# A gated spectral filter and Mish block: GpSimd waits for VectorE's two-input operations, x ahead of w1, gated tiles through ScalarE, and a new order of work

## The chip, the cores and the metric

The kernel runs on one core of one Trainium2 chip. Times are device microseconds of a whole execution; the span is the time from the first to the last instruction in the trace and is about 2 us shorter. TensorE is written PE in the profile (PEld is its weight load), VectorE is DVE, ScalarE is ACT, GpSimd is POOL. A run counts as slow when it lies over 1.5% above the fastest of its kernel, and only fast runs go into a ratio.

## The reference

```python
def reference(A_x, A_w_r, A_w_i, B_x, B_w1, B_b1, B_w2, gate_w):   # x is (1, 2048, 512) bf16
    x = A_x
    g = sigmoid((x * gate_w).sum(-1, keepdims=True))
    X = rfft2(x) * (A_w_r + 1j * A_w_i)          # spectral branch
    a = irfft2(X, s=(2048, 512))
    h = x @ B_w1 + B_b1                          # dense branch: 512 -> 1792 -> 512
    b = (h * tanh(softplus(h))) @ B_w2           # Mish
    return g * a + (1 - g) * b
```

(Abridged. The real text has batch dimensions and casts.)

## The kernel before

The whole kernel is one list of tasks (matmul groups, vector operations, transfers) with declared reads and writes. An order string names the tasks in the sequence in which each engine gets them, the engine where there is a choice, and the PSUM slots. Each engine runs its own tasks strictly in that sequence. `place` turns the declared data into semaphore waits. It knows nothing of the ports that VectorE and GpSimd share; the flag `lock=True` on a task is not read by it.

```python
    def place(self, order):
        ...
        pool_last = None
        ...
        for tok in order.split():
            name, eng, slots = (tok + "::").split(":")[:3]
            ...
            if t.eng == "pool" and not t.isdma:      # GpSimd runs behind itself
                if pool_last is not None and pool_last not in t.deps:
                    t.deps.append(pool_last)
                pool_last = t
            self.order[t.eng].append(t)
```

The dense branch runs in four chunks of 512 rows. A chunk has 14 "bias" matmul groups (x times w1, class mm1), a bias add that empties PSUM (on either engine), exp, ln and tanh on ScalarE, then eight multiplies of h by the tanh (two SBUF inputs), then the second matmul (mm2):

```python
    G.any(f"h{c}_{ft}", [("dve", dve(1024), f_h), ("act", 2 * act(512) + 0.18, f_ha, "b_h")], "h", reads=[b, "b1f"], ...)
    ...
    def f_mul(e, a=a, b_=b_, tl=tl, hb=hb):
        v = hs[hb][:, a:b_, 128 * tl:128 * (tl + 1)]
        return e.tensor_tensor(out=v, in0=v, in1=uv_[:, a:b_, 128 * tl:128 * (tl + 1)], op=ALU.mult)

    G.any(f"mul{c}_{fh}_{tl}", [("dve", dve2(n), f_mul), ("pool", pool(n), f_mul, "b_mul")], "mul", lock=True, ...)
```

The filter weights of the spectral branch need 16 copies of 32 partitions by 2064 elements out of a staging area; in the kernel before all 16 stand on GpSimd. The transposed spectrum (task s1r) is later read back over that staging area, so it waits for all of them:

```python
    G.any(f"{nm}m{fh}{pt}{h}", [("pool", 2.03, f_e), ("dve", 0.71, f_e, "b_rev"), ("act", acts(2064), f_a, "b_rva")],
          "w", off=o, lock=True, reads=rd, writes=[key, ("stg", fh, ri, pt, h)], deps=dp)
    ...
    t_s1r.append(dma(f"s1r{g}", rE[g:128:4, 0:8192], scr_r[32 * g:32 * g + 32, :], ..., deps=t_mv))
```

At the end, ten tiles of the spectral result are added to the dense result on VectorE straight from PSUM:

```python
    def f_fin(e, t=t, b=b):
        return e.scalar_tensor_tensor(out=bs[:, t, :], in0=bank(b), scalar=gcol[:, t:t + 1], in1=bs[:, t, :], op0=ALU.mult, op1=ALU.add)
```

The stretch of the order string around the first chunk's multiplies (`mul0`). `wrm`/`wim` with `:pool` are weight copies on GpSimd, and four of them stand in it:

```
wim111:pool tanh0_0 mm1_1_6::1 zcl0 d10::2 d11 wrm100:pool mm1_1_7 ed10:dve p12::0 p13 h1_6:dve s1w2 mm1_1_10::2 wim100:pool mm1_1_11 ep12:dve
mm1_1_8::1 h1_10:act mul0_0_0:dve d12::0 d13 mul0_0_3:dve mm1_1_9 ez0 mul0_0_1:dve tanh0_8 mm2_0_0_0::0 mul0_0_2:dve ed12:dve wrm001:pool mm2_1_0_0::1
```

## Time and profile before

| | before |
|---|---|
| time before the prediction, median of 3 | 154.35 us (154.17 to 154.51) |
| span of the profiled run | 152.6 us |
| mean granted TensorE clock | 0.966 |
| first multiply of chunk 0 | 41.09 us |
| first spectral matmul over the transposed data | 76.72 us |
| first tanh of the last chunk | 130.55 us |

The lines that carry the reading are in the prediction below. One view is not in it: the busy time of each engine by stretch, cut at the three events of the table. The columns are the window and its length, then busy us (and instructions) of PE, PEld, DVE, ACT and POOL, then granted clock, share of the DMA engines, and GB/s. For the kernel before:

```profile
0.00:41.09 41.09, 36.69 (x280) 21.20 (x285) 29.84 (x32) 26.27 (x21) 26.72 (x23) 1.00 0.96 225
41.09:76.72 35.63, 29.64 (x148) 13.90 (x150) 30.59 (x30) 27.14 (x16) 14.67 (x12) 0.86 0.62 206
76.72:130.55 53.83, 50.71 (x363) 28.50 (x369) 52.25 (x78) 51.69 (x39) 0.53 (x2) 1.00 0.30 73
130.55:152.60 22.05, 18.89 (x117) 11.34 (x116) 17.37 (x25) 7.58 (x3) 0.00 (x0) 1.00 0.23 84
```

The second row is the odd one: TensorE, VectorE and ScalarE are all idle for 5 to 8.5 of its 35.63 us, and it alone has a clock under 1.

### The profile page before, as it was taken

The page shows a single profiled execution, that of the slowest core. Times are in us where ns is not written, and L with a number is a line of the kernel's source. Part 1 is how long each engine was busy: PE and PEld are TensorE (multiplying, and loading weights), DVE is VectorE, ACT ScalarE, POOL GpSimd, SP SyncE. Part 2 cuts the span into 40 slices and gives each one's busy share as a digit, 9 for nine tenths or more (in the row PEclk, how much of TensorE's full clock was granted, in tenths as well). Part 3 has the DMA queues.
Part 4 walks back from the last instruction along what each step waited for, and adds up shares of the span by engine and source line. Part 5 has one row for each costly group of instructions (what it writes and reads, how often), then busy time and mean ns, then how long its engine had stood idle before and what let it go on. Part 6 is the DMA issues. An engine that isn't in the chain of part 4 may idle for free.

```text
span 152.6 us, 2289 instructions
## 1 busy us (share of the span) xinstructions
PE 135.9 (89%) x903; PEld 74.9 (49%) x919; DVE 130.0 (85%) x162; ACT 112.7 (74%) x78; POOL 41.9 (27%) x36
## 2 busy tenths in 40 slices
PE   5799999799975389999999999989898799999991
PEld 3554455457522235544466543434654384764471
DVE  0369598996999995858999999999999899999981
ACT  3411469999990959999359999999999999992000
POOL 3150579999999910005000100000000000000000
PEclk9999999999998558999999999999999999999999
DMA  4999999749910397099997556400000000310233
GB/s 123 325 378 336 162 195 131 118 101 291 331 37 0 83 324 292 10 252 391 410 299 180 118 135 161 105 14 0 0 0 4 0 0 0 137 73 0 103 138 105
DMA packets 22830, 22.37 MB, mean 147 GB/s; under 512 B 13668, under 2 KB 19684, under 8 KB 22372
## 3 DMA queue, kind: packets, MB, share of 16 engines
q1 hardware_dynamic: 22496, 22.00, 53.5%
q10 hardware_dynamic: 324, 0.23, 0.6%
q8 instruction: 7, 0.11, 0.3%
q14 instruction: 3, 0.02, 0.0%
HBM read 14.89 MB, written 4.19 MB: 125 GB/s over the span
## 4 chain that ended last, share of the span: by engine, by line
PE 52%; DVE 38%; issue 4%; DMA 3%; ACT 1%; SPq 0%; DVEq 0%
PE ps L925 23%; PE ps L876 17%; DVE hs L909 9%; PE ps L855 5%; DVE rD L883 4%; DVE rD L503 3%; DVE rF L503 3%; DVE rC L757 3%; DMA rA<-in_A_x_dram 3%; DVE tmp L760 3%; DVE rC L503 2%; DVE hs L883 2%; DVE rD L909 2%; DVE rX L942 2%; PE ps L633 1%
## 5 line engine op out<-in xcount | busy, mean ns | idle before, releaser
L876 PE MATMUL ps<-rX,w_sb 128*128 128x512 bf16 x218 | 51.4, 385 | 1.2 <-DVE rC L503 0.5
L925 PE MATMUL ps<-w_sb,hs 128*128 128x512 bf16 (+1 forms) x176 | 41.6, 383 | 7.0 <-DVE hs L909 5.8
L876 PEld LDWEIGHTS ps<-rX,w_sb 128*128 128x128 bf16 x224 | 21.5, 99 | 25.7 <-issue 1.4
L925 PEld LDWEIGHTS ps<-w_sb,hs 128*128 128x128 bf16 x182 | 17.8, 101 | 26.4 <-DVE hs L909 6.9
L897 ACT ACTIVATE uT<-hs 128x2048 bf16<-128x2048 bf16 (+1 forms) x12 | 20.4, 1696 | 13.0 <-DVE hs L883 7.1
L899 ACT ACTIVATE uT<-uT 128x4096 bf16<-128x4096 bf16 (+1 forms) x8 | 25.5, 3191 | 0.1
L900 ACT ACTIVATE uT<-uT 128x4096 bf16<-128x4096 bf16 (+1 forms) x8 | 25.5, 3190 | 0.1
L883 DVE TENSOR_TENSOR hs<-ps,b1f 128x1024 bf16<-128x1024 f32 x15 | 17.9, 1213 | 2.5 <-PE ps L876 2.4
L909 DVE TENSOR_TENSOR hs<-hs,uT 128x1024 bf16<-128x1024 bf16 (+1 forms) x24 | 19.5, 872 | 0.1
L942 DVE TENSOR_SCALAR rX<-ps,omg 128x512 bf16<-128x512 f32 (+1 forms) x16 | 11.4, 711 | 6.6 <-PE ps L925 6.6
L925 PE MATMUL ps<-w_sb,rD 128*128 128x512 bf16 x53 | 12.9, 379 | 1.5 <-DVE rX L942 0.8
L503 DVE CAST rC<-ps 128x1024 bf16<-128x1024 f32 x9 | 10.9, 1213 | 2.0 <-PE ps L622 1.8
L503 DVE CAST rD<-ps 128x1024 bf16<-128x1024 f32 x8 | 10.3, 1305 | 1.7 <-PE ps L633 1.6
L506 ACT ACTIVATE rC<-ps 128x1024 bf16<-128x1024 f32 x7 | 6.9, 1027 | 4.2 <-PE ps L743 4.2
L503 DVE CAST rA<-ps 128x1024 bf16<-128x1024 f32 x7 | 8.8, 1299 | 0.1
L925 PEld LDWEIGHTS ps<-w_sb,rD 128*128 128x128 bf16 x56 | 5.2, 98 | 7.1 <-DVE rX L942 1.3
L669 POOL TENSOR_SCALAR rW<-rE 32x2064 bf16<-32x2064 bf16 x4 | 8.1, 2024 | 1.4 <-DMA rE<-in_A_w_r_dram 1.0
L608 DVE TENSOR_TENSOR rB<-rA 128x1024 bf16<-128x1024 bf16 (+2 forms) x7 | 4.0, 589 | 5.3 <-DMA rA<-in_A_x_dram 5.3
L506 ACT ACTIVATE rX<-ps 128x512 bf16<-128x512 bf16 x8 | 4.6, 596 | 5.3 <-PE ps L595 5.3
L668 POOL COPY rA<-rE 32x2064 bf16<-32x2064 bf16 x4 | 8.3, 2076 | 0.3
L608 POOL TENSOR_TENSOR rB<-rA 128x1024 bf16<-128x1024 bf16 (+1 forms) x3 | 5.0, 1667 | 11.6 <-DMA rA<-in_A_x_dram 11.6
L669 POOL TENSOR_SCALAR rA<-rE 32x2064 bf16<-32x2064 bf16 x4 | 8.0, 1991 | 0.3
(83 smaller groups left out, 173.1 us busy)
## 6 DMA issues: line engine op xcount, KB each, us to landing
scr<-rD SPq DMA_DIRECT2D x4, 512.0 KB, 4.2
rF<-c_m SPq DMA_DIRECT2D x1, 2048.0 KB, 9.5
rE<-scr SPq DMA_DIRECT2D x4, 512.0 KB, 5.7
rB<-c_g SPq DMA_DIRECT2D x1, 2048.0 KB, 10.4
tmp<-rC SPq DMA_DIRECT2D x16, 128.0 KB, 2.3
out_dram<-rX SPq DMA_DIRECT2D x7, 256.0 KB, 2.0
rA<-in_A_x_dram SPq DMA_DIRECT2D x3, 512.0 KB, 9.3
w_sb<-in_B_w_dram SPq DMA_DIRECT2D x2, 768.0 KB, 9.3
```

Of the source, the lines that this page charges most:

```text
L503: return e.tensor_copy(out=o(), in_=i())
L506: return e.activation(o(), i(), AF.Copy)
L608: return e.tensor_tensor(out=xu[:, a:b_, uv, :], in0=x_sb[:, a:b_, 0:256], in1=x_sb[:, a:b_, 256:512], op=ALU.add if uv == 0 else ALU.subt ...
L669: return e.tensor_scalar(out=o_, in0=i_, scalar1=1.0, scalar2=0.0, op0=ALU.mult, op1=ALU.add)
L876: ins = e.matmul(bank(b, i), w1_sb[:, dt_, 128 * ft:128 * (ft + 1)], xT[:, c, dt_, :, :], start=(dt_ == 0), stop=(dt_ == 3))
L883: return e.tensor_tensor(out=hs[hb][:, ft:ft + 2, :], in0=pair(b).rearrange("p (f s) -> p f s", f=2), in1=b1f[:, ft:ft + 2].unsqueeze(2).t ...
L897: return e.activation(o, hsf[hb][:, 512 * a:512 * b_], fn_)
L899: return e.activation(o, o, fn_, bias=1.0)
L900: return e.activation(o, o, fn_)
L909: return e.tensor_tensor(out=v, in0=v, in1=uv_[:, a:b_, 128 * tl:128 * (tl + 1)], op=ALU.mult)
L925: ins = e.matmul(bank(b)[:, 0:hi - lo], hs[hb][:, ft, 128 * tl:128 * (tl + 1)], w2_sb[:, ft, lo:hi], start=(ft == 0), stop=(ft == NFT - 1))
L942: return e.tensor_scalar(out=bs[:, t, lo:hi], in0=bank(b)[:, 0:hi - lo], scalar1=omg[:, t:t + 1], scalar2=None, op0=ALU.mult)
```

## The change

Its intent is to keep GpSimd and VectorE from needing their shared ports at the same time, to feed the spectral branch earlier, and to take work off VectorE at the end. The order string was made anew to go with it, so it differs nearly everywhere. Cut to its core:

```diff
@@ place
-        pool_last = None
+        pool_last = lock_last = None
...
                 pool_last = t
+                if lock_last is not None and lock_last not in t.deps:
+                    t.deps.append(lock_last)
+                lock_last = None
+            if t.eng == "dve" and t.lock:
+                lock_last = t
@@ ORDER (both strings cut to the multiplies of chunk 0)
-... mul0_0_0:dve d12::0 d13 mul0_0_3:dve mm1_1_9 ez0 mul0_0_1:dve tanh0_8 mm2_0_0_0::0 mul0_0_2:dve ed12:dve wrm001:pool ...
+... mul0_0_0:dve mm1_1_11 mul0_0_2:dve mul0_0_3:dve mm2_0_0_0::0 mul0_0_1:dve mul0_1_1:dve exp1_0 mul0_1_0:dve ... mul0_1_3:dve mm2_0_0_1 h1_10:dve mul0_1_2:pool ...
+... wim101:dve ... wrm011:dve ... wim001:dve ... wim111:dve ... wim010:pool ... wrm001:dve ...
@@ loads
-        ld_x(0); ld_x(1); ld_w1(0); ld_x(2); ld_w1(1); ld_w1(2); ld_x(3); ld_x(4)        # one call a line in the kernel
+        for s in LOADS[loads].split():          # loads=1: "x0 x1 x2 w0 w1 x3 w2 x4"; x0..x2 are x tiles 0 to 7
+            (ld_x if s[0] == "x" else ld_w1)(int(s[1]))
@@ gated tiles (merge: 10 -> 12 tiles kept apart; finb=11 of them in the new way)
+                    if t < finb:
+                        G.add(f"fa{t}", "act", ..., lambda ...: e.activation(tb(z)[:, 0:512], bank(b), AF.Copy, scale=gcol[:, t:t + 1]), ...)
+                        G.any(f"fb{t}", [("pool", pool(512), f_fb), ("dve", dve2(512) + 0.03, f_fb, "b_fb")], ..., lock=True, ...)   # bs += tmp
+                    else:
                         G.add(f"fin{t}", "dve", dve(512) + 0.06, f_fin, "fin", ...)
```

By the new order string, five of the sixteen weight copies run on VectorE, seven more bias adds run on VectorE rather than ScalarE, five output scalings go the other way, six two-input operations move from VectorE to GpSimd, and ten of the eleven gated adds go to VectorE and one to GpSimd.

## The prediction

> **What bounds the kernel now.** I read the page's busy shares and slices first. No engine is full over the whole span (PE 89%, VectorE 85%, ScalarE 74%), so the bound changes by stage, and the slices say where to look: the granted clock falls in one place only.
>
> ```profile
> PE 135.9 (89%) x903; PEld 74.9 (49%) x919; DVE 130.0 (85%) x162; ACT 112.7 (74%) x78; POOL 41.9 (27%) x36
> ...
> PEclk9999999999998558999999999999999999999999
> ```
>
> A slice is 152.6 / 40 = 3.8 us, so the digits 8, 5, 5, 8 cover about 46 to 61 us. I then took the chain of waits around it:
>
> ```profile
> 41.13 8.62 DVE hs L909 x4
> ...
> 51.84 1.65 DVE gcol L730
> ...
> 54.10 5.05 PE ps L925 x12
> ```
>
> Four VectorE multiplies (the activation times tanh, 128x1024 each) take 8.62 us, and a 12-column multiply takes 1.65 us. The timeline of VectorE has the same four multiplies in the last chunk, and the timeline of GpSimd shows what differs:
>
> ```profile
> 41.09 8.66 DVE L909 TENSOR_TENSOR hs<-hs,uT 128x1024 bf16<-128x1024 bf16 x4
> ...
> 134.20 2.50 DVE L909 TENSOR_TENSOR hs<-hs,uT 128x1024 bf16<-128x1024 bf16 x4
> ```
> ```profile
> 42.34 4.56 POOL L668 COPY rA<-rE 32x2064 bf16<-32x2064 bf16 x2
> 46.98 2.23 POOL L669 TENSOR_SCALAR rA<-rE 32x2064 bf16<-32x2064 bf16 x1
> 49.28 4.20 POOL L668 COPY rW<-rE 32x2064 bf16<-32x2064 bf16 x2
> ```
>
> At 134 us GpSimd is empty and the four take 2.50 us. At 41 us GpSimd runs its filter-weight copies, 1.90 us each when undisturbed; each multiply then takes about one such copy more, and the copies stretch to 2.1 to 2.3 us. The two engines take turns. The waits say who pays:
>
> ```profile
> PE ps L925 <- DVE hs L909: 5.8, 2, 3.1
> ACT uT L897 <- DVE hs L909: 5.5, 2, 3.7
> ```
>
> TensorE stands for 5.8 us and ScalarE for 5.5 us. Afterwards TensorE runs at half clock: the 12 matmuls at 54.10 take 5.05 us, 421 ns each, against 14 in 3.02 us (216 ns each) in the chain at 141.10, at full clock.
>
> **What the Trainium skill says.** "SBUF — State Buffer", section "Who interferes with whom", says that a VectorE instruction with two SBUF inputs contends with a GpSimd instruction that reads SBUF, that whoever issues first holds the shared ports for the whole instruction, and that a VectorE instruction with one SBUF input outside the two-port modes doesn't contend. The trace agrees: the bias adds (PSUM and one small SBUF operand) take 1.20 us at 31.41, beside GpSimd copies, and 1.22 us at 80.62 with GpSimd idle. "TensorE: Matmul & The Clock Gate", section "Why this matters for your kernels", asks for no PE gap above about 3 us; the gaps here are 2.72 and 3.11 us and the clock did fall to 0.50 (49.7 to 54.0 us). "GPSIMD Engine Reference", section "Engine selection", calls two-input work about twice as slow on GpSimd; for this bf16 shape the trace says 2120 ns against 681 to 685 ns, three times. "VectorE: DVE Perf Modes", section "The perf-mode tier table", gives bf16 copies in SBUF four elements per cycle; the trace has 1.24 us for 64x4160.
>
> **The change part by part.**
>
> *The semaphore wait.* Each GpSimd instruction now waits for the last VectorE two-input (or weight) operation placed before it. That does not by itself stop a later VectorE operation from running into a GpSimd one; it is the new order that does. After nearly every GpSimd read of SBUF it puts about 2 us of VectorE work that reads PSUM (two bias adds, for instance), as long as the GpSimd instruction lasts. Ten weight copies stand on GpSimd before the first multiply: from 19.9 us (the weights' landing, about unchanged) 10 x 1.97 = 19.7, to about 40 us; the first multiply comes at about 41 us. Of the six left, five go to VectorE: 2064 / 4160 of 1.24 us with its fixed part, about 0.7 us each, 3.4 us together (an estimate; the odd row length is not in this trace).
> Worth: multiplies 8.66 - 2.50 = 6.2 us; the small operations at 50.88 and 51.84, 0.66 + 1.65 less two of 0.16, 2.0 us. That is 8.2 us on VectorE. On TensorE it is idle 2.72 + 3.11 = 5.8, plus half clock (5.05 - 12 x 0.216 = 2.5, and 2.64 - 8 x 0.216 = 0.9): 9.2 us. VectorE heads the chain and TensorE follows; I count 9 us, and take 1 us back for collisions that remain.
>
> *Who does what.* Counted from the order, with durations from start to start (bias add 1.14, spectral evictions 1.14 to 1.22, output scaling 0.66, 1024-column multiply 0.605, 768-column 0.48). VectorE: +7 bias adds (+8.0), +5 copies (+3.4), +2 inverse evictions (+2.3), -3 forward evictions (-3.5), -5 output scalings (-3.3), -6 two-input operations to GpSimd (-3.4), and gated adds below (-2.4): about +1 us, from some 120 uncontended to 121. ScalarE up to its last tanh: 7 bias adds away (7 x 1.17 = -8.2), two inverse evictions away (-1.9), three forward ones in (+2.9), five output scalings in (+3.0), one gated tile (+0.6): -3.6 us. ScalarE has no idle over 0.2 us from 80.98 to 138 except 0.2 at 104.4, so this is worth having only because VectorE can take it: 2 to 3 us. Also the forward spectrum is finished before the first multiply rather than at 63.7 us, so ScalarE's 3.90 us wait at 77.8 for the next spectral matmuls should shrink: 1 us.
>
> *x tiles 0-7 ahead of w1.* x landed to 0.5 MB at 5.56 us, and 1.5 MB (x0, x1, w1 first part, x2) at 8.85 us. With x2 and w1 swapped, x2 lands near 7 and w1 near 8.9, where the first bias matmuls began (8.82). TensorE does four transposes and two spectral tiles in that time and isn't interrupted by transposes at 18.5 to 23.5. Some 0.5 us later for the first exp, about 2 us of ScalarE copies moved out of the exp stage into its idle 8.1 to 14.8: near 0 in sum.
>
> *Gated tiles.* The words say GpSimd adds them; the order gives 10 of the 11 adds to VectorE. Each replaces a 0.67 us PSUM operation by a ScalarE copy (0.6) and a 512-column SBUF add, about 0.36 us (from 0.605 and 0.48): 9 x 0.31 less, one gone to GpSimd, hence -2.4 with one tile kept as before and one more tile. ScalarE has room: it stands idle from 138 us on. But from 135.3 to 149.6 us TensorE is full (14.2 us for the last four tiles and nine spectral products, 65 x 0.216 = 14.0), and it has 15 us of such work in the new order. So this part is worth nothing at the very end, 0 to 1 us before it.
>
> Sum on the span: 152.6 - 9 + 1 - 2.5 - 1 - 0.5 = 140.6. Timed runs lie 1.75 us over the span (154.35 against 152.6): 142.4, say 142.5 us.
>
> A check by VectorE alone: from 41 us to the last chunk's first multiply it has about 75 us of work in the new order; at before's idle share in the same stretch (some 8%) that is 81, so 122; TensorE's 15, a bubble of 0.6 and the output's 3 us make 140.6.
>
> **The rivals.** (1) VectorE becomes the bound and eats it: it gets the bias adds and copies, while its busy share was already 16.8 of 17 us from 87 to 104. If the weight copies run at one element per cycle (about 2.2 us), they cost 7.5 us more in the very stretch that is to be freed, and the time would be 148 to 150. For: odd rows of 129, reversed. Against: the 1.24 us row. (2) The wait moves: GpSimd, held back, finishes the weights later, and the read of the transposed spectrum, which overwrites their staging, waits. Before, that read was issued at 64.2 us; by my count the last weight is done near 55 us, so there are 9 us of slack. If it bites: 145 to 147. (3) The contention was hidden: everything after 60 us is limited by transfers or TensorE anyway. Against: TensorE was busy 14.8 of 15 us from 72 to 87, and transfers idle from 104 to 120. Then 150 to 154. (4) The slower start: w1's first part at 11 us instead of 9 would cost 1 to 2 us.
>
> **Range and chances.** All three engines meet the last chunk within about 2 us of each other in my count, so stalls add rather than hide; a better packed order could also give 139. Range 138 to 148. Over 2% faster means under 151.3, which needs only a third of the contention to come back: 0.92; within 2%: 0.06; slower: 0.02.
>
> **What would show it.** Right: the first chunk's multiplies at 0.6 us each, no granted clock below 0.9 after the start, PE's wait for the multiplies under 1 us, GpSimd copies at 1.9 us, VectorE copies of weights at 0.7 us, the last tanh some 12 us earlier than 136.96. Wrong: a multiply still near 2 us, weight copies over 1.2 us on VectorE, the spectral matmuls waiting on the read of the transposed spectrum, or a TensorE gap of 3 us elsewhere with the clock falling again.

## The result, and the profile after

The changed kernel took 143.94 us (median of 4 runs, 143.0 to 145.94, the highest of them slow) against 154.43 us for the kernel before in the same rounds (4 runs, 154.17 to 154.82). A ratio here is the mean time of one kernel's fast runs over that of the other's fast runs of the same rounds, so not quite the ratio of the medians: it is 0.9298, with a 95% interval of 0.9247 to 0.9349. All outputs were correct, here and in every run below. The predicted 142.5 us (138 to 148) holds the result.

From the page of the changed kernel, the busy shares, the granted clock and the chain of waits:

```profile
PE 133.1 (94%) x917; PEld 74.5 (52%) x917; DVE 123.7 (87%) x161; ACT 116.2 (82%) x81; POOL 42.0 (30%) x39
...
PEclk9999999999999999999999999999999999999999
...
PE 72%; ACT 20%; DMA 3%; DVE 1%; issue 1%; SPq 0%; ACTq 0%
```

The dip in the clock is gone, and VectorE has all but left the chain that ends last; its share there was 38% before. The same stretches as before, cut at the same three events:

```profile
0.00:43.62 43.62, 38.96 (x323) 23.82 (x324) 33.63 (x35) 28.75 (x22) 25.27 (x23) 1.00 1.05 240
43.62:68.60 24.98, 24.98 (x117) 11.31 (x116) 23.71 (x32) 24.53 (x13) 6.64 (x9) 1.00 0.72 225
68.60:118.51 49.91, 48.97 (x359) 27.77 (x358) 48.75 (x67) 47.86 (x33) 8.89 (x7) 1.00 0.33 83
118.51:141.80 23.29, 20.15 (x124) 11.55 (x121) 17.56 (x30) 15.01 (x15) 1.15 (x1) 1.00 0.25 91
```

Row by row the lengths differ by +2.53, -10.65, -3.92 and +1.24 us, which is -10.8 in all. Some work has moved between the rows with the new order, so they are a guide and not a proof, but the second row speaks clearly: TensorE is busy for all 24.98 us of it, where it had been idle for 6 and at half clock for part of the rest. VectorE's timeline and then GpSimd's show why (start, us, engine, line, operation, and in brackets the idle time before it and what ended that; the line numbers shift by a few between kernels because the text above them grew):

```profile
43.62 4.07 DVE L912 TENSOR_TENSOR hs<-hs,uT 128x1024 bf16<-128x1024 bf16 x7
...
50.07 0.70 DVE L671 COPY rA<-rE 32x2064 bf16<-32x2064 bf16 x1
...
54.87 0.16 DVE L733 TENSOR_TENSOR gcol<-ez,omg 128x12 f32<-128x12 f32 x1
```
```profile
38.15 3.91 POOL L672 TENSOR_SCALAR rA<-rE 32x2064 bf16<-32x2064 bf16 x2
47.83 1.64 POOL L912 TENSOR_TENSOR hs<-hs,uT 128x768 bf16<-128x768 bf16 x1 [5.77 <-DVE hs L912]
53.06 1.91 POOL L672 TENSOR_SCALAR rA<-rE 32x2064 bf16<-32x2064 bf16 x1 [3.58 <-DVE rA L672]
```

Seven multiplies take 4.07 us (0.58 each). GpSimd stands still for 5.77 us just then, released by the last of them; it starts at 47.83, while VectorE empties PSUM. The small operation that took 1.65 us takes 0.16. A weight copy takes 0.70 us on VectorE and 1.91 on GpSimd. One collision remains, in the third chunk: three 768-column multiplies that start at 101.83 us take 2.68 us beside a GpSimd multiply that started at 101.52, where four of them take 1.96 at 127.27 with GpSimd empty. The gain can be read again near the end, on ScalarE. These are the tanh operations of the last chunk, first of the kernel before, then of the changed one:

```profile
130.55 6.41 ACT L900 ACTIVATE uT<-uT 128x4096 bf16<-128x4096 bf16 x2
```
```profile
118.51 3.62 ACT L903 ACTIVATE uT<-uT 128x4096 bf16<-128x4096 bf16 x1
...
124.48 2.75 ACT L903 ACTIVATE uT<-uT 128x3072 bf16<-128x3072 bf16 x1
```

The first half starts 12.0 us earlier. The second ends at 127.23 instead of 136.96, 9.7 us earlier, because the new order puts an eviction, an output scaling and a gated tile (1.30 + 0.67 + 0.69 us by the timeline) between the halves.

### The profile page after: what moved, and what is told of

It is laid out like the page before. It is cut to its first block, busy times and chain, and to the rows that moved or that the text cites. A ratio compares the mean times of both kernels' runs of the same rounds, so it can differ in the third digit from the quotient of the medians.

```text
span 141.8 us, 2331 instructions
## 1 busy us (share of the span) xinstructions
PE 133.1 (94%) x917; PEld 74.5 (52%) x917; DVE 123.7 (87%) x161; ACT 116.2 (82%) x81; POOL 42.0 (30%) x39
## 4 chain that ended last, share of the span: by engine, by line
PE 72%; ACT 20%; DMA 3%; DVE 1%; issue 1%; SPq 0%; ACTq 0%
PE ps L879 34%; PE ps L928 26%; ACT uT L900 5%; ACT uT L902 5%; ACT uT L903 5%; DMA rA<-in_A_x_dram 3%; PE ps L746 3%; PE ps L625 2%; PE ps L636 2%; PE ps L954 2%; ACT rD L515 2%; PE ps L598 2%; PE ps L716 1%; DVE rD L512 1%; ACT L903 1%; ACT L902 1%
## 5 line engine op out<-in xcount | busy, mean ns | idle before, releaser
L928 PE MATMUL ps<-w_sb,hs 128*128 128x512 bf16 (+1 forms) x182 | 39.3, 363 | 0.0
L886 DVE TENSOR_TENSOR hs<-ps,b1f 128x1024 bf16<-128x1024 f32 x21 | 25.2, 1219 | 1.9 <-PE ps L879 1.7
L912 DVE TENSOR_TENSOR hs<-hs,uT 128x1024 bf16<-128x1024 bf16 (+1 forms) x22 | 12.2, 616 | 0.4 <-ACT uT L903 0.3
L945 DVE TENSOR_SCALAR rX<-ps,omg 128x512 bf16<-128x512 f32 (+1 forms) x11 | 7.6, 701 | 3.6 <-PE ps L928 3.4
L512 DVE CAST rC<-ps 128x1024 bf16<-128x1024 f32 x8 | 9.6, 1217 | 0.4 <-PE ps L625 0.3
L962 ACT ACTIVATE tmp<-ps,gcol 128x512 bf16<-128x512 f32 x11 | 7.1, 685 | 3.1 <-PE ps L954 2.4
L966 POOL TENSOR_TENSOR rX<-rX,tmp 128x512 bf16<-128x512 bf16 x1 | 1.2, 1152 | 27.8 <-ACT tmp L962 27.8
L512 DVE CAST rF<-ps 128x1024 bf16<-128x1024 f32 x8 | 9.1, 1208 | 0.0
L886 DVE TENSOR_TENSOR rD<-ps,b1f 128x1024 bf16<-128x1024 f32 x7 | 8.4, 1219 | 0.5 <-PE ps L879 0.5
L512 DVE CAST rD<-ps 128x1024 bf16<-128x1024 f32 x6 | 7.5, 1305 | 1.0 <-PE ps L636 1.0
```

What stands on the lines that cost most here:

```text
L512: return e.tensor_copy(out=o(), in_=i())
L886: return e.tensor_tensor(out=hs[hb][:, ft:ft + 2, :], in0=pair(b).rearrange("p (f s) -> p f s", f=2), in1=b1f[:, ft:ft + 2].unsqueeze(2).t ...
L928: ins = e.matmul(bank(b)[:, 0:hi - lo], hs[hb][:, ft, 128 * tl:128 * (tl + 1)], w2_sb[:, ft, lo:hi], start=(ft == 0), stop=(ft == NFT - 1))
L945: return e.tensor_scalar(out=bs[:, t, lo:hi], in0=bank(b)[:, 0:hi - lo], scalar1=omg[:, t:t + 1], scalar2=None, op0=ALU.mult)
L962: G.add(f"fa{t}", "act", act(512) + 0.09, lambda e, t=t, b=b, z=z: e.activation(tb(z)[:, 0:512], bank(b), AF.Copy, scale=gcol[:, t:t + 1]) ...
```

## The experiments

Twelve experiments ran, with nine different kernels, in three calls. All kernels of a call share a chip and the runs of the kernel before.

My theory was that collisions on the shared ports cost some 9 us, that the new order (and not the wait) removes them, and that moved work gives 2 to 3 us more. The rival explanations were: the wait removes the collisions and the order adds little; the moved work is the gain; or the earlier x loads are.

In the first call the kernel before had a median of 154.17 us in seven runs (151.74 to 154.97). One run at 151.74 makes all the others count as slow by the 1.5% rule, so there is no ratio for this call; I compare the medians within it and say where the choice matters.

### 1. The changed kernel again

No edit: it is the base line of the call.

> The changed kernel itself, for a reference on this chip. Expected 143 to 145 us, as before; no granted clock under 0.9 after the start.

Measured: 143.52 us (142.69 to 144.42), 10.65 below the kernel before of the same call. The first result stands.

### 2. The old order with the wait alone

```diff
 # kernel before; ORDER, loads and gated tiles untouched
-        pool_last = None
+        pool_last = lock_last = None
...
                 pool_last = t
+                if lock_last is not None and lock_last not in t.deps:
+                    t.deps.append(lock_last)
+                lock_last = None
+            if t.eng == "dve" and t.lock:
+                lock_last = t
```

> The kernel before with the semaphore wait alone, its old order kept. My prediction says that the order and not the wait keeps the engines apart: then most of the loss stays, 149 to 153 us, multiplies of the first chunk still near 2 us. Rival: in the old order too ten weight copies end before the first multiply, and the wait alone holds the eleventh back until the fourth multiply is done: then the four take 2.5 us, the clock stays up, and nearly all of the 9 us come back, 145 to 147 us.

Measured: 145.49 us (144.63 to 146.07), 8.7 below the kernel before (6.3 below its one run at 151.74) and only 2.0 above the changed kernel. By medians a few lines of `place` do four fifths of the work, which is what the rival that credits the wait says. VectorE's timeline, then GpSimd's, of this kernel:

```profile
40.04 2.50 DVE L914 TENSOR_TENSOR hs<-hs,uT 128x1024 bf16<-128x1024 bf16 x4
...
43.66 0.94 DVE L732 TENSOR_SCALAR gcol<-ez 128x12 f32<-128x12 f32 x1
```
```profile
42.67 1.90 POOL L673 COPY rW<-rE 32x2064 bf16<-32x2064 bf16 x1 [3.14 <-DVE hs L914]
47.08 3.87 POOL L673 COPY rA<-rE 32x2064 bf16<-32x2064 bf16 x2 [2.51 <-DVE hs L914]
```

The four multiplies take 2.50 us where they took 8.66, to the hundredth what the prediction read from the last chunk. GpSimd's idle time before each of its copies ends with a multiply: it is held for 3.14 and 2.51 us and then runs undisturbed (1.90 us) beside VectorE's evictions from PSUM. In the kernel before, the eleventh copy had started at 40.38 us, ahead of the first multiply at 41.09, though it stands behind the four multiplies in the order string: nothing held it. The wait does not keep a later VectorE operation from running into a copy, and one does (0.94 us rather than 0.16), but that costs 0.8 us, not 8. All 16 copies stay on GpSimd here and are still done at 57 us. So my sentence that the wait "does not by itself stop" the collisions and that "it is the new order that does" is refuted in its second half. The start must be set apart: in this run the first bias matmuls were at full clock from 8.8 us (0.22 to 0.25 us apart, against 0.43 in the trace of before), so the first exp came 1.0 us earlier and with it the first multiply. From the first multiply to the end it is 103.1 us here and 111.5 in the kernel before: the wait is worth 8.5 us there.

### 3. The new order without the wait

```diff
 # changed kernel, order and all else kept
-                if lock_last is not None and lock_last not in t.deps:
-                    t.deps.append(lock_last)
-                lock_last = None
-            if t.eng == "dve" and t.lock:
-                lock_last = t
```

> The changed kernel without the semaphore wait, its new order kept. If the order alone does it: 143.5 to 145 us, the first chunk's multiplies at 0.6 us. If the wait is needed as well: GpSimd's multiply of the first chunk starts at 46.2 us with VectorE's and each takes turns (some 1.6 us lost), and its three filter products start as soon as their data land and cost VectorE up to 2 us each: 146 to 150 us.

Measured: 151.05 us, in four runs of 149.66, 152.45, 147.71 and 153.07; the two highest count as slow. By medians that is 3.1 below the kernel before. Fast runs against the one fast run of the kernel before it is 3.1 as well (148.7 against 151.74), and 5.2 above the changed kernel (143.5). VectorE's timeline of this kernel, then GpSimd's:

```profile
44.84 7.22 DVE L907 TENSOR_TENSOR hs<-hs,uT 128x1024 bf16<-128x1024 bf16 x7
...
85.69 2.40 DVE L761 TENSOR_TENSOR rC<-rC,tmp 128x1024 bf16<-128x1024 bf16 x1
```
```profile
47.46 2.00 POOL L907 TENSOR_TENSOR hs<-hs,uT 128x768 bf16<-128x768 bf16 x1 [3.56 <-ACT uT L898]
49.55 2.10 POOL L667 TENSOR_SCALAR rA<-rE 32x2064 bf16<-32x2064 bf16 x1
```

Without the wait GpSimd is released by the tanh instead of by the multiplies, falls into the middle of them, and the seven take 7.22 us instead of 4.07. A filter addition at 85.69 takes 2.40 us instead of 0.69, beside a GpSimd multiply at 85.57. The order alone does not keep the engines apart. The scatter of 5.4 us fits that small shifts in time decide whether two operations meet, but I have the trace of only one of the four runs, so that is argued and not shown.

The medians of this kernel are too scattered to say how far the two parts overlap. The traces say more, from the first multiply to the end (table after experiment 4): without the wait the old order takes 8.5 us longer than with it, the new order 4.2 us (102.4 against 98.2). So in the one run traced the new order by itself avoids about half of the loss.

### 4. The five weight copies back on GpSimd

```diff
 # changed kernel, order string
-... zcl0 wim101:dve ... wrm011:dve s1w3 wim001:dve ... wim111:dve ... wrm001:dve ...
+... zcl0 wim101:pool ... wrm011:pool s1w3 wim001:pool ... wim111:pool ... wrm001:pool ...
```

> The changed kernel with its five VectorE weight copies given back to GpSimd. VectorE has 3.5 us less to do; GpSimd ends its copies near 61 us instead of 55, so the read of the transposed spectrum is issued at about 62 us instead of 58.4. If there is slack as I predicted (first spectral matmul at 68.6 us unmoved): 143 to 144.5 us. If the read bites: the first spectral matmul at 70 to 72 us and the time 145 to 148 us.

Measured: 151.26 us (150.3 to 151.55), 7.7 above the changed kernel of the call. VectorE's timeline, then TensorE's:

```profile
60.63 1.24 DVE L684 TENSOR_SCALAR rA<-rA 64x4160 bf16<-64x4160 bf16 x1 [1.81 <-POOL rA L672]
65.64 1.24 DVE L683 COPY rW<-rW 64x4160 bf16<-64x4160 bf16 x1 [3.77 <-POOL rW L671]
```
```profile
68.85 1.74 PE L879 MATMUL ps<-rX,w_sb 128*128 128x512 bf16 x4 [4.01 <-DVE rD L886]
...
76.59 0.61 PE L746 MATMUL ps<-rE,rF 128*128 128x128 bf16 x8
```

The duplications of the weights (64x4160) stand early in VectorE's sequence and wait for GpSimd's copies. The bias adds behind them wait too, TensorE gets no free PSUM for 4.01 us, and its next matmuls start 435 ns apart (1.74 / 4), half clock (the trace records 0.50 from 69.0 to 72.5 us). The first spectral matmul comes 8.0 us later than in the changed kernel. Of these, 2.1 were lost before the first multiply (45.73 against 43.62), where nothing was edited: in this run the first bias matmul came at 13.03 us and the clock record begins at 14.43, against 11.37 and 10.79. The copies account for the other 5.9 in this trace. So the five moves are needed by this order, and the trace shows the wait in VectorE's own sequence. The read of the transposed spectrum is late too (issued at 65.63 instead of 58.36), so the second rival of the prediction, with its "9 us of slack", was set aside on a count that holds only for the copies as placed; what the late read would cost by itself no run shows. In the old order with the wait all 16 copies fit on GpSimd.

The kernels of the call and the kernel before side by side (us into the profiled run; then the span, the part of it from the first multiply on, and the median time):

| | first multiply | first spectral matmul | first tanh, last chunk | span | from first multiply | time |
|---|---|---|---|---|---|---|
| before | 41.09 | 76.72 | 130.55 | 152.6 | 111.5 | 154.17 |
| wait only | 40.04 | 66.77 | 121.16 | 143.1 | 103.1 | 145.49 |
| order and the rest, no wait | 44.84 | 72.54 | 123.93 | 147.3 | 102.4 | 151.05 |
| both | 43.62 | 68.60 | 118.51 | 141.8 | 98.2 | 143.52 |
| both, copies on GpSimd | 45.73 | 76.59 | 126.50 | 149.8 | 104.1 | 151.26 |

(The traces of before and of both are those of the first result; the profiled run of the changed kernel in this call differs by at most 0.2 us in these events.) The column from the first multiply on is the steadiest measure: the first result and experiments 1, 5, 6, 9, 10, 11 and 12 have the same order from the first multiply on, and in all eight traces it takes 98.21 to 98.23 us. So in these eight runs all the difference in span lies before the first multiply. In the old order with the wait the first spectral matmul even comes earlier than in the new one, 66.77 against 68.60, because the new order reaches its first multiply 3.6 us later. From the first multiply on the new order is 4.8 us shorter, most of it (4.5) between the first spectral matmul and the last chunk's tanh.

### 5 and 10. The first bias matmuls ahead of the transposes of x tiles 4 to 7

```diff
 # changed kernel, loads=2 ("x0 x1 w0 x2 w1 x3 w2 x4") and the head of the order string
-... evx1:act bf4_1:dve wr1s0 p2::2 p3 tr7::0 ... tr4::1 ... tr6::0 p4::0 ... tr5::1 ... tr_b::0 ... mm1_0_2::1 ...
+... evx1:act wr1s0 p2::2 p3 ep0:dve tr_b::0 ... mm1_0_0::0 ... mm1_0_1 ... mm1_0_2::1 tr7::1 ... tr4::0 ... tr6::1 ... tr5::0 p4::0 p5 ...
```

> The changed kernel with another start: w1's first part is loaded ahead of x tiles 4-7, and the first bias matmuls stand before the transposes of tiles 4-7 and their spectral tiles on TensorE. If those transposes, paced by ScalarE's evictions, are what moved the first bias matmul from 8.8 to 11.4 us, it starts near 9 us, and as TensorE heads the chain up to 98 us some 1 to 2.4 us come off: 141 to 142.5 us. If the later start is made good elsewhere anyway: 143 to 144 us.

> The kernel with the early first bias matmuls again. Its first five bias matmuls started 0.4 us apart (half clock), which ate the early start. Expected the same as before, 142.3 to 143.3 us, 0.5 to 1.2 us under the changed kernel.

Measured: 142.79 us (141.51 to 143.62) in the second call, ratio 0.9257 (0.9204 to 0.9309), where the kernel before had 154.49; and 143.63 us (143.21 to 144.42) in the third, ratio 0.9343 (0.9302 to 0.9385), beside the changed kernel at 145.6 there (experiment 9). In the third call that is 2.0 us by medians and 1.5 by the ratios, whose intervals just miss each other. TensorE's timeline of the changed kernel, then of this one:

```profile
11.37 12.26 PE L879 MATMUL ps<-rX,w_sb 128*128 128x512 bf16 x56
```
```profile
8.81 3.76 PE L879 MATMUL ps<-rX,w_sb 128*128 128x512 bf16 x12
```

The first bias matmul comes 2.56 us earlier and the first exp 1.4 (16.58 against 18.02), but the first chunk's matmuls end at 23.24 instead of 23.46 us and the first multiply starts at 43.40 instead of 43.62. In the third call it is the same: 43.67 against 43.79, and the two profiled runs took 143.81 us each. So the traces show 0.1 to 0.2 us; the rest of the difference comes from the other five runs of the changed kernel in that call (144.83 to 146.27), which left no trace. The transposes that the changed kernel does first have to be done in either case, and the early matmuls are slow: twelve take from 8.81 to 12.40, 299 ns each, against 216 ns for the 56 in the line above it (23.46 less 11.37, over 56). The view gives a granted clock of 1.00 throughout, but the traces of experiments 5 and 10 hold no clock record at all; the spacing of the first six (0.40 to 0.43 us) says that it was half.

### 11. The same with 15 warm-up matmuls instead of 9

```diff
 # kernel of experiment 10
-        NWARM = 9
+        NWARM = 15
```

> The same with 15 warm-up matmuls instead of 9 (TensorE is idle there until x lands at 5.5 us). If the slow first bias matmuls are the clock that hasn't come up, they start 0.216 us apart, the first chunk's bias matmuls end about 1 us earlier (22.2 instead of 23.2 us) and the time is 0.5 to 1 us less, 141.5 to 142.5 us. If they wait for w1's landing: no change.

The Trainium skill ("TensorE: Matmul & The Clock Gate", section "What's actually happening") says that the warm-up is a matter of time, about 3.4 us, and not of the number of matmuls. In the changed kernel the nine take 2.10 us, in this one the fifteen take 3.38. TensorE's timeline of this kernel:

```profile
8.22 2.76 PE L879 MATMUL ps<-rX,w_sb 128*128 128x512 bf16 x11
```

Measured: 141.79 us (141.46 to 141.85, 4 runs), ratio 0.9215 (0.9175 to 0.9255), 3.8 below the changed kernel's median of the same call and 1.8 below experiment 10. The order has twelve matmuls here (one record is missing), and they take from 8.22 to 10.82, 217 ns each. The first multiply starts at 41.80 instead of 43.62 and the last chunk's tanh at 116.71 instead of 118.51: 1.8 us won at the start are kept to the end. Its clock record begins with 1.00 at 4.96 us, 3.8 us after the first warm-up matmul; in the changed kernel it begins at 10.79. This agrees with the page, and it shows that the slow early matmuls of experiment 5 were an unwarmed clock. It is the best version, ahead of both kernels. The longer warm-up without the early bias matmuls was not tried, so the share of each in the 1.8 us is not separated beyond what experiment 10 shows.

### 6 and 12. The load order alone

```diff
 # changed kernel, loads=2: w1's first part before x tiles 4 to 7
-... braw ident x2 graw w1_0 w1_1 x3 ...
+... braw ident graw w1_0 x2 w1_1 x3 ...
```

> The changed kernel with only x tiles 4-7 and w1's first part swapped back in the load order, the instruction order kept. If the load order is worth what I predicted (near 0): 143.5 to 144.3 us, the first bias matmul at 11.4 to 12 us. If x's early landing is what the new start rests on: 1 us or more later, 144.5 to 146 us.

> The changed kernel with only the load order of x tiles 4-7 and w1's first part swapped back, again, since its six runs spread over 3.4 us. If the load order costs by itself: 1 to 1.8 us over the changed kernel of this call. If that was scatter: within 0.7 us of it.

Measured: 145.31 us (143.84 to 147.2; three of six runs slow), ratio 0.939 (0.9316 to 0.9464); and 144.33 us (143.72 to 146.85), ratio 0.9388 (0.9343 to 0.9432), where the changed kernel of the same call has 0.9438 (0.9386 to 0.949). The intervals overlap: the swap of the two loads by itself cannot be told from nothing. The profiled runs show how uneven the start is. The first bias matmul came at 11.57 us in the one and at 13.19 us in the other of these two runs of the same kernel, the transposes of the late x tiles having started at 9.02 and 9.54 us. Eight of them take 0.62 us in the one and 1.03 in the other, so part of the difference is again a clock that was warm in one run and not in the other (the record of the second begins at 13.34 us; the first has none). What makes the landing of x and the early clock vary from run to run stays open.

### 9. The changed kernel a third time

No edit: the base line of the third call.

> The changed kernel once more, so that the three runs beside it are compared on one chip: 143 to 144.5 us.

Measured: 145.6 us (143.81 to 146.27), ratio 0.9438 (0.9386 to 0.949), with the kernel before at 153.69. On this chip the gain is 5.6%, on the first 7.0%. The size of the gain is known to about one and a half percentage points across chips.

### 7. The gated tiles on VectorE as before

```diff
 # changed kernel, finb=0: each fa in the order becomes fin, and each fb goes
-... fa10::0 mul3_0_1:dve ... fa4::1 fb10:dve ... fb0:pool ...
+... fin10 mul3_0_1:dve ... fin4 ...
```

> The changed kernel with the gated tiles as before, one VectorE operation out of PSUM each in the place of the ScalarE copy. Mine: TensorE is full at the end, so it is worth 0 to 1 us: 143.5 to 144.6 us. Rival: the 3 us less on VectorE all count, 146 us and more.

Measured: 145.86 us (144.94 to 146.42), ratio 0.945 (0.9402 to 0.9498). There was no changed kernel in this call. Against its ratios in the other calls (0.9298 and 0.9438) the loss is between 0.2 and 2.3 us, so the time alone does not size it; the trace does. First from its waits between 122 and 150 us (what waits and for what, us in total, times, longest), then from VectorE's timeline:

```profile
PEld ps L953 <- DVE rX L957: 1.9, 4, 1.1
...
PE ps L953 <- DVE rX L957: 0.6, 1, 0.6
```
```profile
134.44 3.38 DVE L957 SCALAR_TENSOR_TENSOR rX<-ps,gcol,rX 128x512 bf16<-128x512 f32 x5
```

VectorE works the gated tiles off one behind the other at 0.66 us, and TensorE's products for the next tiles wait for the PSUM that they hold. From the first tanh of the last chunk to the end it is 24.8 us (118.93 to 143.7) against 23.3 in the changed kernel: 1.5 us. The timed runs lie 2.3 to 2.5 us over their spans here and 1.8 to 2.1 in the changed kernel, so some 0.5 us more is lost outside the span. In the changed kernel's own waits of that stretch this wait does not appear.

### 8. The seven bias adds back on ScalarE

```diff
 # changed kernel, order string: seven tasks
-h1_12:dve h1_10:dve h1_8:dve h2_8:dve h3_10:dve h3_6:dve h3_4:dve
+h1_12:act h1_10:act h1_8:act h2_8:act h3_10:act h3_6:act h3_4:act
```

> The changed kernel with seven bias adds given back to ScalarE (1.17 us each, 8.2 us). Mine: ScalarE heads the chain up to the last tanh, so most of it shows, 146 to 150 us. Rival: VectorE, 8 us lighter, is the tighter engine: 142 to 144 us.

Measured: 149.81 us (149.18 to 150.44), ratio 0.971 (0.9653 to 0.9768). ScalarE's timeline of this kernel:

```profile
125.38 3.62 ACT L903 ACTIVATE uT<-uT 128x4096 bf16<-128x4096 bf16 x1
```

The last chunk's first tanh comes 6.9 us later than in the changed kernel, and the span is 6.9 us longer (148.7 against 141.8). Seven bias adds at the 1.17 us that the prediction took from the kernel before are 8.2 us, so nearly all of it lands on the end: in this order ScalarE's sequence sets most of the time up to the last tanh. The figure holds for this order: the old order with the wait has those adds on ScalarE and is only 2 us slower in all.

## Why the prediction was right, and where it was not

**The collisions and their price: right.** The sum put 9 us less 1 on them. The wait alone brings 8.7 us by medians and 8.5 from the first multiply to the end of the traces, with the multiplies at 2.50 us for four as read from the last chunk, the small operations at 0.16 but for one, and no gap over 1 us and no half clock on TensorE in that stretch (its 512-column matmuls stay 0.22 us apart; the trace has no clock record).

**Which part removes them: wrong.** The step that failed is "That does not by itself stop a later VectorE operation from running into a GpSimd one; it is the new order that does." The first clause holds as a statement about what the wait can do, but it was taken for the size of the effect. In the old order the six copies that collided all stand behind the four multiplies and had only run ahead of their place, so holding them back was enough (experiment 2: 8.5 us), and the new order without the wait still loses 4.2 us in its trace (experiment 3). I had looked for what could still go wrong after a GpSimd instruction started, and not at which instructions had started before their turn. The total came out right because both parts were in the change.

**Who does what: right in direction, the parts mis-sized.** I took VectorE's busy time from some 120 uncontended to 121; it is 122.7 with the wait alone and 123.7 in the changed kernel, so the difference of 1 holds. Everything but the wait is worth 2.0 us beside it by medians (145.49 to 143.52), where the terms of the sum, - 2.5 - 1 - 0.5, gave 4.0. By the traces it is worth 4.8 us from the first multiply on, and a start that is 3.6 us later gives most of that back (part of the 3.6 is the early clock of experiment 2's run). The bias adds alone are worth more than the 2 to 3 us (6.9 in the trace of experiment 8, in this order), so the other moves cost something too.

**Weight copies on VectorE: right in cost, for the wrong reason.** They take 0.70 us each, as estimated, so the first rival is out. Without those moves this order loses 5.9 us after the first multiply (experiment 4), through the operations that queue behind the copies on VectorE. The read of the spectrum, the second rival, is 7.3 us late there too, so the slack that I counted is gone; whether it alone would have bitten is not shown.

**x ahead of w1 and the start: mis-sized.** I had 0.5 us later for the first exp and near 0 in sum. The first exp starts at 18.02 us instead of 14.80, 3.2 us later, and the first multiply 2.5 us later. The weights too reach GpSimd at 22.24 us and not at the 19.9 that I took as unchanged. The load order by itself cannot be told from nothing (experiments 6 and 12). Putting the first bias matmuls ahead of the four transposes moves the first multiply by 0.1 to 0.2 us in the traces (experiments 5 and 10); with a warm clock as well it moves by 1.8 (experiment 11). I had not looked at the clock of the start at all. What makes up the rest of the later start is open. So the fourth rival, a slower start, came true beside the gain.

**Gated tiles: mis-sized.** I had "nothing at the very end, 0 to 1 us before it"; the trace of experiment 7 gives 1.5 us, and it lies after the first tanh of the last chunk. I had counted TensorE as full there and VectorE's time as free. In a full stretch TensorE still needs empty PSUM, and who empties it sets its pace.

**The tests.** Multiplies at 0.6 us, no clock under 0.9 after the start, GpSimd copies at 1.9 and VectorE copies at 0.7 all held, and TensorE no longer waits for the multiplies in the changed kernel. The last tanh is 9.7 us earlier, not 12, for the work put between its halves.

## What to carry to other kernels

Where two engines share a port, ask which instructions of one stand behind the other's burst in the order and are yet free to start before it: one wait that holds them behind the burst may give nearly all the gain, and it can be tried alone before any reordering. A copy moved between two in-order engines changes what stands behind it in both sequences, so count the operations that queue behind its consumer, and not only the transfer that waits for it. Compare runs from a fixed event on as well as by their totals: here that took the uneven start out of the comparison. An earlier start on TensorE was worth 0.2 us with a cold clock and 1.8 with a warm one, and in a stretch where TensorE is full the engine that empties PSUM sets the pace.

## What the Trainium skill lacked or had wrong

- "GPSIMD Engine Reference", section "Engine selection", gives about twice VectorE's time for two-input work. For 128x1024 bf16 operands the trace of the changed kernel has 1.97 us on GpSimd (at 82.95 us, undisturbed) against 0.69 on VectorE, close to three times, so the figure does not hold for this shape and type.
- "TensorE: Matmul & The Clock Gate", section "Seeing it yourself", warns that throttle events in a trace can be unreliable. It does not say that they can be missing: five of the fourteen traces here (experiments 2, 5, 6, 8 and 10) hold none, and the view then prints 1.00, for experiment 5 too, whose first matmuls started 0.40 to 0.43 us apart. Where there are records they fit the spacing: in the kernel before it falls from 0.43 to 0.22 us at 10.95 us, and the record begins at 10.97.
- "TensorE: Matmul & The Clock Gate", section "Why this matters for your kernels", sets the limit of a gap at about 3 us. Here a gap of 2.72 us in the kernel before (it ended at 47.50) was already followed by a clock of 0.50 from 48.5 us, before the second gap began at 50.99; in experiment 8 a gap of 2.67 us was not, its next matmuls starting 0.22 us apart.
- "Vector Engine (DVE) Microarchitecture Reference", section "Performance modes — why throughput varies by op and dtype", lists operands with a negative step as not measured. The weight copies have 16 rows of 129 elements a partition, half of them read backwards: forward (COPY) and backward (TENSOR_SCALAR) copies both take 0.70 us on VectorE and 1.9 us on GpSimd.
